# Moving three DMA groups and one cast in a fused attention and feed-forward kernel

## The chip, the cores and the metric

The kernel runs on 1 core of a Trainium2 chip. The metric is the device time of one execution in microseconds (us). A run is described by the median of several executions; one further execution is recorded by the profiler, and its span (first to last instruction) is what the views of the profile divide up.

The core's engines run their own instruction streams in order and wait for each other by semaphores: PE (matrix products; PEld is its weight load), DVE (vector), ACT (activation functions and copies), POOL (casts here) and SP, which in this kernel issues almost all DMA transfers.

## The reference, cut to what matters

```python
# q, k, v: (8, 8, 576, 64) float32; chunks of 64 rows attend to themselves
scores = scale * q_c @ k_c.T ;  attn = softmax(scores) ;  out = attn @ v_c
x = out.transpose(0, 2, 1, 3).reshape(4608, 512)
h = x @ w_in                      # (4608, 2048)
g = 0.5 * h * (1 + erf(h / sqrt(2)))
y = g @ w_out                     # (4608, 512)
```

## The kernel before

**Tiles.** The 4608 rows are cut into nine tiles of 512 rows, `t` = 0 to 8: one per batch entry (its first 512 rows), and a ninth of the 64 rows that are left of each. A tile's path is: load q, k, v; cast to bf16 on POOL; transpose q and k by DMA; scores, exp, product with v and division (attention); transpose x; mm1 (x times `w_in`, then Gelu); mm2 (times `w_out`); store.

**Rounds.** `phase(t, e1, e2)` runs mm1 and then mm2 of tile t. In the dictionaries `e1` and `e2` work on later tiles is hung at named places of it: during round t the attention of tile t + 1 ends (`rows_av`, `rows_x`), the scores of tile t + 2 are made (`quad_S`), and q, k, v of tiles t + 2 and t + 3 are loaded and cast. "Fifth and sixth mm1" are rounds t = 4 and t = 5. All order is written out by hand (`tc.manual_schedule()`): each engine executes in the order in which the program names the instructions.

**Fewer products.** From t = 1 in mm1 and from t = 3 in mm2 the product is done in seven block products instead of eight (a Strassen-Winograd scheme). The sums of blocks that it takes are DVE instructions: `w_in_sums` (L573, L579 to L582) for the weights, `x_sums` (L588, L598) for x, and for h: `h_sums` (L552, L553), `h_third` (L557) and `h_fourth` (L561).

**mm1 from t = 4 to 7** follows the word list `FOUR` (L620) in `mm1_groups`. A digit and a group letter is a block product (four matmuls, L658). `c1`, `c2`, `c3` and `a1`, `a2` are copies of PSUM sums and additions to them (L693, L706, L709) and `g..` the Gelus (L665). The word `c3c` allocates an output-sized tile from `ypool` (L702) for one of these sums, and DVE fills it at L706 (`h_sb<-h_Y`). `ypool` has two buffers under one tag, and mm2 takes two of them per round for its output, `y[0]` and `y[1]`. So the tile of `c3c` in round t + 1 sits in the buffer of `y[0]` of round t, and L706 waits until the stores from `y[0]` have landed.

**mm2 from t = 3** is `mm2_seven` (L742). Its places, in order: `also(0)`; X product; `also(1)`; `h_third`; products into Y; first store (`y[0]`, left half, L773); `h_fourth`; `also(2)`; the product of `s[3]` by `T[3]` into Z (L778) in two halves, with `also((2, 0))` behind the first; second store (`y[1]`, right half, L780); `also(3)`; a product into Y; third store (`y[0]`, right half, L784); `also(4)`; last product; fourth store (`y[1]`, left half, L788). Each store is one DMA issued on SP (L827).

**DMA.** Loads of k are four DMAs of 256 KB (L102), for tile 8 eight DMAs of 128 KB (L106). V is loaded by `load_v_rows` (L115) in two halves by the parity of the head: four DMAs for parity 0 and five for parity 1 (L122); `cast_v_rows` (L200, L206) casts them by one POOL instruction each. `flip` (L189) transposes q or k by DMA, `rows_x` flips x in two parts (L336). SP issues in program order. The program's semaphores for DMA go round eight at a time: each DMA also waits until the eighth DMA before it has landed.

Of the kernel before, what the change touches and what calls it, by code (L numbers as in the profile page):

```python
# [11 lines left out]
def kernel(  # L12
# [15 lines left out]
    B, H, S, D = q.shape  # L28
# [39 lines left out]
    w_t, w_s = {}, {}  # L68
# [46 lines left out]
    def load_v_rows(t, parity=range(2)):  # L115

        if "vf" not in tiles[t]:
            tiles[t]["vf"] = stage_tile()[:].rearrange("p (h n d) -> p h n d", h=H, d=D)
        raw = tiles[t]["vf"]

        def go(to, rows):
            nc.sync.dma_start(to, rows.rearrange("h key d -> key h d"))  # L122
        last = CT // 2 - 1
        if t < B and 0 in parity:
            for n in range(CT // 2):
                go(raw[:, 0::2, n], v[t, 0::2, P * n:P * (n + 1), :])
        if t < B and 1 in parity:
            for n in range(last):
                go(raw[:, 1::2, n], v[t, 1::2, CH + P * n:CH + P * (n + 1), :])
            go(raw[0:CH, 1::2, last], v[t, 1::2, MT - CH:MT, :])  # L130
            go(raw[CH:P, 1::2, last], v[t, 1::2, 0:CH, :])
        if t == B:
            for b in range(B):
                for r in parity:
                    c, n = place(r, b)
                    go(raw[CH * c:CH * (c + 1), r::2, n], v[b, r::2, MT:S, :])
# [60 lines left out]
        DV(st["kt"][:, g * J:(g + 1) * J].rearrange("p n (e j) -> p (n e) j", j=J),  # L197
           raw[:, g * J:(g + 1) * J].rearrange("p j e -> p e j"))

    def cast_v_rows(t, copy):  # L200
        st = tiles[t]
        st["v"] = ld.tile([P, H, CT // 2, D + 1], bf16, tag="v", name="v_nat")
        if t >= FIRSTX:
            nc.gpsimd.memset(st["v"][:, :, :, D:], 1.0)
        for r in range(2):
            copy(st["v"][:, r::2, :, :D], st["vf"][:, r::2])  # L206
# [122 lines left out]
    def rows_x(t):  # L329

        st = tiles[t]
        rows = work.tile([P, G * CT // 2, 2, D], bf16, tag="x_t", name="x_r", bufs=1)
        xT = st["x"][:].rearrange("p g (n e) -> p (g n) e", e=P)

        def flip_rows(b0, b1):
            nc.sync.dma_start_transpose(xT[:, b0:b1], rows[:, b0:b1].rearrange("p b r d -> p (b r d)"))  # L336
        for bank in range(6):
            b0 = NX * (bank // 2)
            ni = min(NX, G * CT // 2 - b0)
            av = st["av"][bank][:, :ni]  # L340
            one = work.tile([P, NX], f32, tag="one", name="one", bufs=2)
            nc.vector.reciprocal(one[:, :ni], av[:, :, D])
            to = rows[:, b0:b0 + ni, bank % 2]
            nc.vector.tensor_tensor(to, av[:, :, :D], one[:, :ni].to_broadcast([P, ni, D]), op=mybir.AluOpType.mult)
            if bank == 1:
                flip_rows(0, NX)
        flip_rows(NX, G * CT // 2)
# [218 lines left out]
    def w_in_sums(kk, groups):  # L566

        w = in_blocks()
        if not w_s:
            own = consts.tile([P, 4, 2, 4, 2, P], bf16, name="w_in_s")  # L570
            w_s["all"] = own
            for n, g in enumerate("abcd"):
                for i in range(4):  # L573
                    w_s[g, i + 1] = own[:, i, :, n]
        TT, add, sub = nc.vector.tensor_tensor, mybir.AluOpType.add, mybir.AluOpType.subtract
        ns, q, e = {"ab": (slice(0, 2), slice(0, 2), 0), "c": (2, 0, 2), "d": (3, 1, 2)}[groups]
        a11, a12, a21, a22 = (w[:, c, kk, r, q, e:e + 2] for r in range(2) for c in range(2))
        s1, s2, s3, s4 = (w_s["all"][:, i, kk, ns] for i in range(4))
        TT(s1, a21, a22, op=add)  # L579
        TT(s2, s1, a11, op=sub)  # L580
        TT(s3, a11, a21, op=sub)
        TT(s4, a12, s2, op=sub)  # L582
# [128 lines left out]
    def w_sums(which):  # L711

        b11, b12 = w_out_sb[:, :FH, :NH], w_out_sb[:, :FH, NH:]
        b21, b22 = w_out_sb[:, FH:, :NH], w_out_sb[:, FH:, NH:]
        for i in (1, 3):
            if i in which:
                pair = wsum.tile([P, 2, FH, NH], bf16, tag="wsum", name="w_t")
                w_t[i], w_t[i + 1] = pair[:, 0], pair[:, 1]
        of = {1: (b12, b11), 3: (b22, b12), 2: (b22, w_t[1]), 4: (b21, w_t.get(2))}
        for i in which:  # L720
            nc.vector.tensor_tensor(w_t[i], *of[i], op=mybir.AluOpType.subtract)
# [172 lines left out]
    def pool_cast_qk(t):  # L894
        pool_cast_q(t)
        pool_cast_k(t)
# [38 lines left out]
    with tc.manual_schedule():  # L935
# [98 lines left out]
        def flips_of(n):  # L1034
            for nm in "qk":
                flip(n, nm)
# [5 lines left out]
        def loads_of_qk(n):  # L1042
            for nm in "qk":
                load_qk(n, nm)
# [14 lines left out]
        for t in range(1, NT):  # L1059
            e1, e2 = {}, {}  # L1060
            n = t + 1
            if n < NT:
                tiles[n]["x"] = xpool.tile([P, G, MT], bf16, tag="x", name="x")
            if t == 1:
                flips_of(2)
                load_v_rows(2, (1,))
                cast_v_rows(2, PO)
                loads_of_qk(3)
                pool_cast_qk(3)
                e1 = {"1a": [lambda: w_in_sums(slice(0, 2), "c")], "p": [lambda: load_v_rows(3)], "end": [lambda: w_sums((1, 3))]}  # L1070
                e2 = one_tile(2, {5: [lambda: act_table(Act.Gelu)],
                                  8: [lambda: flips_of(3), lambda: loads_of_qk(4)]})
            elif t == 2:
                cast_v_rows(3, PO)
                pool_cast_qk(4)
                e1 = {f"i{g}": [lambda g=g: in_order(3, g)] for g in range(G)}
                e1.update({f"w{i}": [lambda i=i: w_sums((i,))] for i in (2, 4)})
                flips_of(4)
                load_v_rows(4)
                load_qk(5, "q")  # L1080
                cast_v_rows(4, PO)
                e2 = one_tile(3, {8: [lambda: load_qk(5, "k")], 14: [lambda: quad_S(4)]})
            elif n < NT:
                def ahead(t=t):
                    if FIRST7 < t < B - 2:
                        load_v_rows(t + 2)
                    if t + 2 < NT:
                        flips_of(t + 2)
                    if t == FIRST7:
                        load_ahead(t, "q")  # L1090
                    if t == B - 1:
                        load_v_rows(B, (1,))
                        cast_v_rows(B, PO)

                def late_v(t=t):
                    load_v_rows(t + 2)
                    cast_v_rows(t + 2, PO)

                def behind(t=t):
                    load_ahead(t, "k")  # L1100
                e1 = {"begin": [ahead]}
                if t + 2 < NT:
                    e1["begin"] = [lambda t=t: pool_cast_k(t + 2), ahead]
                if t + 2 == B:
                    def behind_sums(t=t):
                        nc.gpsimd.tensor_copy(tiles[B]["q"][:, 0, 0, 0, 0:1], tiles[t]["s", 2][:, 0, 0:1])
                        pool_cast_q(B)
                        pool_cast_k(B)
                        ahead()
                    e1 = {"g11b": [behind_sums]}  # L1110
                if t == FIRST7:
                    pool_cast_q(t + 2)
                    e1["tab"] = [lambda: act_table(Act.Gelu)]
                e2 = {1: [lambda: rows_av(n, tiles[n - 1]["Z"]), lambda: rows_x(n)], 2: [], 3: [], 4: [behind, lambda: x_sums(n)]}
                if t == FIRST7:
                    e2[2] += [late_v, lambda: w_in_sums(slice(0, 2), "d")]
                if FIRST7 < t < B - 2:
                    e2[1] += [lambda t=t: cast_v_rows(t + 2, PO)]
                if t == B - 2:
                    e2[1] += [lambda: load_v_rows(B, (0,))]  # L1120
                if t + 3 < NT:
                    if t > FIRST7:
                        e2[1] += [lambda t=t: load_ahead(t, "q")]
                    if t + 3 < B:
                        e2[1] += [lambda t=t: pool_cast_q(t + 3)]
                if n + 1 < NT:
                    e2[1] = [lambda: act_table(Act.Exp)] + e2[1]
                    e2[2 if t == FIRST7 else (2, 0)] = e2[2] + [lambda: quad_S(n + 1), lambda: act_table(Act.Gelu)]
            phase(t, e1, e2, between=last_rows if t == 1 else {})
# [28 lines left out]
```

## Time and profile before

| what | us |
|---|---|
| runs | 272.81, 273.38, 275.05 |
| median of these | 273.38 |
| profiled execution, whole | 275.35 |
| its span | 273.5 |
| PE busy in it | 262.0 |
| DVE busy | 196.5 |
| ACT busy | 185.6 |
| POOL busy | 79.0 |

Matmuls are pipelined, so a matmul's length in the profile is longer than the time it adds; a row of the timeline with four matmuls of 128x256 advances by 0.44 us. The timeline view gives start, length, engine, line, operation, output and inputs, and in brackets how long the engine stood idle before the row and what ended that.

### The profile page before, as it was taken

What the parts mean: (1) busy time and instruction counts of PE and PEld (TensorE: products, weight loads), DVE (VectorE), ACT (ScalarE), POOL (GpSimd) and SP (SyncE); (2) the same over time, 40 slices, a digit from 0 to 9 for tenths busy, and PEclk for the clock granted to TensorE, in tenths of its full rate; (3) what the DMA queues carried; (4) which work ended last, traced back from release to release, by engine and by line L of the source; (5) the groups of instructions that cost most, each with busy time, mean ns of one, the idle gap of its engine ahead of it and who ended that gap; (6) DMA issues with size and microseconds to landing.
All of it is one profiled execution on the core that took longest, in us unless ns stands there. A gap on an engine that the chain in (4) does not pass through costs nothing. (4 is left out here: it accounts for less than half of the span.)

```text
span 273.5 us, 7503 instructions
## 1 busy us (share of the span) xinstructions
PE 262.0 (96%) x3040; PEld 194.6 (71%) x3057; DVE 196.5 (72%) x360; ACT 185.6 (68%) x361; POOL 79.0 (29%) x125
## 2 busy tenths in 40 slices
PE   8799999999999999999999999999999999999993
PEld 2474455467447754678888888888887888888782
DVE  2547574898895999479958965995599559946841
ACT  3438674887967875997679767966895699338600
POOL 2634666450650361430434203510061011000000
PEclk9759999999999999999999999999999999999999
DMA  6999999998969979989999989979977571440005
GB/s 190 267 357 405 395 396 248 244 266 205 319 174 250 263 161 200 281 205 200 239 236 257 217 228 277 210 141 151 238 180 131 115 213 27 76 157 2 1 2 155
DMA packets 128628, 56.60 MB, mean 207 GB/s; under 512 B 104016, under 2 KB 123472, under 8 KB 128592
## 3 DMA queue, kind: packets, MB, share of 16 engines
q1 hardware_dynamic: 128272, 55.59, 80.1%
q8 instruction: 24, 0.39, 0.6%
q10 hardware_dynamic: 320, 0.52, 0.5%
q14 instruction: 12, 0.10, 0.1%
HBM read 36.70 MB, written 9.44 MB: 169 GB/s over the span
## 5 line engine op out<-in xcount | busy, mean ns | idle before, releaser
L658 PEld LDWEIGHTS <-w_in_s 128*128 128x128 bf16 x448 | 43.7, 98 | 7.0 <-issue 0.4
L658 PEld LDWEIGHTS <-w_in_sb 128*128 128x128 bf16 x336 | 32.8, 98 | 6.7 <-issue 0.6
L727 PEld LDWEIGHTS <-h_s 128*128 128x128 bf16 x304 | 29.3, 98 | 4.7 <-DVE h_s L557 1.2
L836 PE MATMUL y_ps<-w_out_sb,h 128*128 128x512 bf16 x137 | 31.4, 379 | 1.0 <-issue 1.0
L156 POOL CAST q_nat<-arrival 128x512 bf16<-128x512 f32 x33 | 20.2, 649 | 39.6 <-DMA arrival<-in_q_dram 38.1
L658 PE MATMUL h_X<-x,w_in_sb 128*128 128x256 bf16 x224 | 31.4, 273 | 0.0
L156 POOL CAST k_nat<-arrival 128x512 bf16<-128x512 f32 x34 | 23.4, 722 | 27.6 <-DMA arrival<-in_k_dram 22.9
L658 PE MATMUL h_Y<-x_t,w_in_s 128*128 128x256 bf16 x224 | 31.1, 272 | 0.2 <-ACT h_a L706 0.2
L727 PEld LDWEIGHTS <-h 128*128 128x128 bf16 x288 | 28.2, 98 | 3.7
L206 POOL CAST v_nat<-arrival 128x1024 bf16<-128x1024 f32 x14 | 15.9, 1136 | 48.1 <-DMA arrival<-in_v_dram 48.1
L727 PE MATMUL y_ps<-w_t,h_s 128*128 128x256 bf16 x208 | 25.1, 273 | 0.7 <-DVE h_s L557 0.7
L836 PEld LDWEIGHTS <-h 128*128 128x128 bf16 x144 | 13.4, 98 | 15.2 <-issue 0.2
L727 PE MATMUL y_ps<-w_out_sb,h 128*128 128x256 bf16 x192 | 22.9, 273 | 0.0
L693 ACT COPY h_Y<-h_X 128x512 f32<-128x512 f32 x28 | 15.8, 581 | 9.8 <-PE h_X L658 9.7
L933 ACT ACT_TABLE_LOAD x16 | 20.5, 1283 | 1.0 <-PEq L1142 0.7
L706 DVE COPY h_a<-h_Y 128x512 f32<-128x512 f32 x8 | 5.5, 690 | 18.1 <-PE h_Y L658 18.1
L665 ACT ACTIVATE h<-h_Y 128x512 bf16<-128x512 f32 x28 | 16.5, 594 | 1.7 <-PE h_Y L658 1.3
L665 ACT ACTIVATE h<-h_X 128x512 bf16<-128x512 f32 x28 | 16.7, 600 | 1.4 <-PE h_X L658 0.8
L235 ACT ACTIVATE pT<-s_ps 128x512 bf16<-128x512 f32 x28 | 14.4, 602 | 4.6 <-PE s_ps L228 4.6
L658 PE MATMUL h_Z<-x_t,w_in_s 128*128 128x256 bf16 x112 | 16.8, 273 | 0.0
L658 PE MATMUL h_Y<-x,w_in_s 128*128 128x256 bf16 x112 | 16.4, 272 | 0.0
L658 PE MATMUL h_Z<-x_t,w_in_sb 128*128 128x256 bf16 x112 | 16.4, 272 | 0.0
(146 smaller groups left out, 495.2 us busy)
## 6 DMA issues: line engine op xcount, KB each, us to landing
out_dram<-y_sb SPq DMA_DIRECT2D x32, 256.0 KB, 3.2
arrival<-in_q_dram SPq DMA_DIRECT2D x7, 1024.0 KB, 6.9
arrival<-in_k_dram SPq DMA_DIRECT2D x24, 256.0 KB, 5.7
arrival<-in_v_dram SPq DMA_DIRECT2D x42, 128.0 KB, 3.0
arrival<-in_moe_w_out_dram SPq DMA_DIRECT2D x4, 1024.0 KB, 12.2
arrival<-in_v_dram SPq DMA_DIRECT2D x8, 256.0 KB, 6.2
arrival<-in_moe_w_in_dram SPq DMA_DIRECT2D x4, 512.0 KB, 6.8
arrival<-in_moe_w_in_dram SPq DMA_DIRECT2D x2, 1024.0 KB, 10.6
```

The lines of the kernel that those rows point to most:

```text
L156: copy(st[nm][:, g].rearrange("p j r d -> p r j d"), st[nm + "f"][:, 2 * g:2 * g + 2])
L206: copy(st["v"][:, r::2, :, :D], st["vf"][:, r::2])
L235: nc.scalar.activation(pT[:].rearrange("p u (c j) -> p u c j", j=J), s_ps[g2][c][:].rearrange("p u (j c) -> p u c j", j=J), Act.Exp, scale ...
L658: nc.tensor.matmul(banks[g + name][:, i], lhs[:, kk, i], rhs[:, kk], start=fresh and i == kk == 0, stop=(kk == 1), skip_group_check=True)
L665: nc.scalar.activation(h[:, j:j + 2, m], src[:], Act.Gelu)
L693: AC(banks[g + "Y"][:], banks[g + "X"][:])
L706: (AC if i == 0 else DV)(sums[g, i][:], banks[g + "Y"][:])
L727: nc.tensor.matmul(out[m], lhs[:, f, m * P:(m + 1) * P], rhs[:, f, :], start=fresh and f == 0 and (m == 0 or len(out) == 3), stop=(f == FH ...
L836: nc.tensor.matmul(y_ps[:], st["h"][:, f, ms * P:(ms + 1) * P], w_out_sb[:, f, :], start=(f == 0), stop=(f == FF - 1))
L933: nc.scalar.activation(act_scratch[:], rest[:, 0:1], func)
```

## The change

Three edits:

1. Round 1: the cast of V of tile 2, the loads of q and k of tile 3 and their casts are named after `w_in_sums(..., "c")` instead of at the head of the round. The cast of V is made to wait for those sums by a copy of one column of `w_in_s` into `v_nat` ahead of it on POOL. By this the loads of q and k also stand behind the store of the last row block of tile 0 on SP.
2. Rounds 4 and 5: only the first half of V of tile t + 2 is loaded ahead of the DMA transposes of q and k; the second half (five DMAs) follows them.
3. Rounds 3, 4 and 5: the loads of k of tile t + 3 (`behind`) are hung at `also(3)` instead of `also(4)`, and so are issued behind the second store of the round and ahead of the third.

```diff
-    def cast_v_rows(t, copy):
+    def cast_v_rows(t, copy, behind=None):
         st = tiles[t]
         st["v"] = ld.tile([P, H, CT // 2, D + 1], bf16, tag="v", name="v_nat")
+        if behind is not None:
+            copy(st["v"][:, 0, 0, 0:1], behind)
...
             if t == 1:
                 flips_of(2)
                 load_v_rows(2, (1,))
-                cast_v_rows(2, PO)
-                loads_of_qk(3)
-                pool_cast_qk(3)
-                e1 = {"1a": [lambda: w_in_sums(slice(0, 2), "c")], "p": [lambda: load_v_rows(3)], "end": [lambda: w_sums((1, 3))]}
+                def behind_sums():
+                    w_in_sums(slice(0, 2), "c")
+                    cast_v_rows(2, PO, w_s["c", 4][:, 0, 0, 0:1])
+                    loads_of_qk(3)
+                    pool_cast_qk(3)
+                e1 = {"1a": [behind_sums], "p": [lambda: load_v_rows(3)], "end": [lambda: w_sums((1, 3))]}
...
                 def ahead(t=t):
                     if FIRST7 < t < B - 2:
-                        load_v_rows(t + 2)
+                        load_v_rows(t + 2, (0,))
                     if t + 2 < NT:
                         flips_of(t + 2)
+                    if FIRST7 < t < B - 2:
+                        load_v_rows(t + 2, (1,))
...
-                e2 = {1: [lambda: rows_av(n, tiles[n - 1]["Z"]), lambda: rows_x(n)], 2: [], 3: [], 4: [behind, lambda: x_sums(n)]}
+                e2 = {1: [lambda: rows_av(n, tiles[n - 1]["Z"]), lambda: rows_x(n)], 2: [], 3: [behind], 4: [lambda: x_sums(n)]}
```

## The prediction, made before the changed kernel ran

> **What bounds the kernel now.** I read the page first (who is busy), then the windows of rounds 4, 5 and 6, then the waits of PE and its weight load, then timelines of DVE, POOL, PE and SP where rounds differ.
>
> ```profile
> PE 262.0 (96%) x3040; PEld 194.6 (71%) x3057; DVE 196.5 (72%) x360; ACT 185.6 (68%) x361; POOL 79.0 (29%) x125
> ```
>
> PE leaves 11.5 us of the span idle, nearly all of it before 45 us, which the change does not touch. Each window below runs from one round's first matmul to the next one's; the first number after the stretch is its length, then PE.
>
> ```profile
> 136.20:162.40 26.20, 26.18 (x354) 23.05 (x352) 19.92 (x40) 19.94 (x38) 6.79 (x10) 1.00 1.01 225
> 162.40:189.20 26.80, 26.44 (x354) 23.00 (x353) 20.39 (x39) 20.68 (x38) 7.36 (x11) 1.00 0.91 211
> 189.20:215.95 26.75, 26.41 (x354) 23.01 (x353) 20.21 (x39) 20.65 (x38) 5.93 (x10) 1.00 0.86 172
> ```
>
> The same 354 matmuls take 26.20, 26.80 and 26.75 us: rounds 5 and 6 lose 0.60 and 0.55 us. The waits view and the timelines say where:
>
> ```profile
> PEld L727 <- DVE h_s L557: 1.2, 2, 0.6
> ...
> 151.62 0.69 DVE L553 TENSOR_TENSOR h_s<-h_s,h 128x1024 bf16<-128x1024 bf16 x1
> ...
> 177.18 0.68 DVE L552 TENSOR_TENSOR h_s<-h 128x1024 bf16<-128x1024 bf16 x1
> 177.90 1.41 DVE L553 TENSOR_TENSOR h_s<-h_s,h 128x1024 bf16<-128x1024 bf16 x1
> ...
> 177.29 1.48 POOL L206 CAST v_nat<-arrival 128x1024 bf16<-128x1024 f32 x1 [1.56 <-DMA arrival<-in_v_dram]
> ...
> 185.18 1.05 PE L727 MATMUL y_ps<-w_t,h_s 128*128 128x256 bf16 x8 [0.34 <-DVE h_s L557]
> ```
>
> In round 5 V's second cast starts at 177.29 inside L552, takes 1.48 us instead of 1.04, and L553 takes 1.41 instead of 0.69 (round 4). DVE is 0.72 late from there, h_third (L557) ends late, and PE waits for it at 185.18. Round 6 has the same with the casts of k: L553 0.98 and L552 0.82 instead of 0.69 and 0.42, and a wait of the same kind. So up to 0.60 + 0.55 = 1.15 us can be won here.
>
> What can be lost stands on SP and DVE at the end of round 5 and in round 6:
>
> ```profile
> 185.36 4.90 SPq L111 DMA_DIRECT2D arrival<-in_q_dram  x8
> 190.68 1.69 SPq L827 DMA_DIRECT2D out_dram<-y_sb  x3
> 192.93 7.18 SPq L106 DMA_DIRECT2D arrival<-in_k_dram  x8
> 200.21 0.57 SPq L827 DMA_DIRECT2D out_dram<-y_sb  x1
> ...
> 199.53 0.68 DVE L706 COPY h_sb<-h_Y 128x512 f32<-128x512 f32 x1
> 200.31 0.69 DVE L709 TENSOR_TENSOR h_sb<-h_Z,h_sb 128x512 f32<-128x512 f32 x1
> 201.15 0.69 DVE L706 COPY h_d<-h_Y 128x512 f32<-128x512 f32 x1
> 201.94 0.69 DVE L709 TENSOR_TENSOR h_d<-h_Z,h_d 128x512 f32<-128x512 f32 x1
> ...
> 202.69 0.60 PE L658 MATMUL h_Z<-x_t,w_in_sb 128*128 128x256 bf16 x4
> ```
>
> L706 at 199.53 (word c3c) refills the buffer of y[0]; in the built programs, before and after, it waits for round 5's first and third stores. Before, the third is issued at 192.00 and lands 5.6 us later, at 197.6: slack 1.9 us. Between L706 and the matmuls at 202.69 DVE has no spare time but 0.15 us ahead of 201.15.
>
> **Part 2, V's second half behind the transposes (rounds 4, 5).** No instruction is added. In round 5 the first half is issued from about 169 to 171.9, the transpose of q follows (1.90 us before) without waiting for five loads, that of k waits for the end of k's cast (174.7 before, about 174 after), then five loads take 2.8 us, to about 179. A V load lands 2.7 to 4.1 us after issue (median 3.0), so the second cast starts at about 181.5 instead of 177.29. There DVE runs rows_x, which reads PSUM; a cast beside it in round 4 (153.42) left both at their usual lengths. The 0.72 us on DVE and PE's wait go: 0.60 less 0.05 that stays (round 5 has a small wait at 175.94 from h1's L553, which meets k's cast), **-0.55 us**. Low end 0 if the cast lands on h_third, high end -0.60. x's flips on SP start when rows_x has made x (181.7 before), behind loads that are out by 179: free. In round 4 the moved loads end at about 154.6, just ahead of x's first flip (154.93 before); landing at 157 or later, the cast meets h_third (156.91 to 158.13) after its start and delays h_fourth, which has 0.6 us spare before its product: 0, at worst +0.7 if it starts just ahead of h_third.
>
> The rows say that one of the two waits: the cast's extra 0.44 us is what L552 had left at 177.29 (to 177.86, less the overlap of one DVE row with the next, about 0.1), and L553 ends 0.7 after the cast. The Trainium skill (SBUF — State Buffer, Who interferes with whom) has it as an exclusive lock: a DVE instruction with two SBUF inputs and a GpSimd one that reads SBUF block each other for a whole instruction. The trace agrees with its 1.48 and 1.41; by that rule, too, the one-PSUM-input rows_x is free, and a cast just ahead of h_third would cost a whole 1.04 us there, less 0.35 us of slack.
>
> **Part 3, k one store sooner (rounds 3, 4, 5).** k lands sooner by what one store takes of the queue, about 0.7 us; POOL's casts of k start that much sooner, PE needs them a round later: 0. But the third store now stands behind the k loads. Round by round, on the clock of before:
>
> - Round 3 into 4: SP is issue-bound there; four k loads take 3.45 us (row at 140.03), so the third store goes from 139.56 to 142.95 and lands just ahead of where the fourth landed (147.6): about 146.7. c3c of round 4 is due at 146.49: 0.2 late, less 0.15: **+0.1**, bounds 0 and +0.9 (at 147.6).
> - Round 4 into 5: from 163.93 to 166 or 167, landing at 171.5 (it must land before the fourth, 172.7), due at 173.02: 0.
> - Round 5 into 6: the tile-8 loads wait for q, eight DMAs back. The third store and first three k loads started at 192.00, 192.93, 193.92, 194.97, each as a q load landed. After, k loads 1 to 4 take these four starts; the last one is 0.87 long, and loads 5 to 8 at the median of 0.63 end at 198.4 (at their own former lengths 199.4). The third store follows: 198.4 to 199.4. Since rows_x, the flips and q move 0.7 sooner, 197.7 to 198.7. Landing 2.9 us later, as the fourth did behind the k loads at 200.21: 200.6 to 201.6. c3c is due at 199.53 - 0.55 = 199.0. Late by 1.6 to 2.6; I take 2.1, less 0.15, **+1.95**. Bounds: landing after 2.3 us (shortest store of the trace) and starting at 197: 0.3 late; at the former landing of the fourth store, 203.1, which stood behind the same transfers: 4.1 late on paper, 3.6 if that moves with the rest.
>
> A transfer issued later moving later is also what the Trainium skill says (DMA: Bandwidth & Descriptors, Queues, rings and completion order): on each DMA engine descriptors are consumed in ring order. The rows agree: the four stores of round 5 landed in the order of issue, behind q.
>
> With DVE 2 us late in round 6, its h sums meet no k casts, which the gate on h1 (L1106, 199.74) starts ahead of the wait: **-0.45** of the 0.55.
>
> **Part 1, round 1.** The copy costs POOL 0.19 us (row L1106). V's first cast moves from 57.98 to about 60.5; before, it stretched the fourth x sum to 1.14 from 0.41 us. PE's small waits there (0.14 us at 59.57, 0.08 at 60.09) end with copies on ACT, not DVE, so I take 0; bounds -0.3 and +0.2. Behind the cast on POOL are q and k of tile 3, which wait for loads until 70.7. The store goes 2.5 us sooner, the 1 MB loads of q and k 0.7 later; their transposes are issued at 80.98, 4 us after k's cast: 0.
>
> **Sum.** -0.55 + 0.1 + 0 + 1.95 - 0.45 + 0 = +1.05, and 0.1 for k's casts meeting h1 in round 5: +1.15. The profiled execution took 275.35 (273.5 and 1.85 around it), 1.97 over the median of 273.38; it would become 276.5, the median **274.5**.
>
> **The rivals.**
>
> - *Faster: the third store of round 5 still lands in time.* One point decides: its landing against 199.0. It needs an issue by 196.1 at 2.9 us. For: eight loads of bare 0.6 us from 191.3 end at 196.1. Against: four of them wait for q. Then -0.55 - 0.5 and the rest 0: 272.4.
> - *Several stores late and a cast on h_third:* 3.4 in round 6, 0.7 in round 4 and no gain in round 5: about +3.3, 276.7. For: 5.6 us is how long the store took before; against: that was with q's megabyte ahead of it.
> - *Nothing to see:* the wait in round 6 is 0.8 and pays off the two gains: 273.4. For: the low end 0.3; against: it needs the shortest landing and earliest issue together.
>
> **How the numbers follow.** Forecast (late by 1.3 to 3) 0.62; faster rival 0.16; nothing 0.12; worse rival 0.10. The forecast's own range is 273.9 to 275.6; to leave out 2 in 10 the range reaches from 272.5 to 276.0. A measurement of this kernel can tell about 1% (2.7 us) from no change: faster by that needs more than the 1.15 us that can be won, 0.03; slower is the worse rival and a little of the forecast, 0.12; within 1% 0.85.
>
> **What would show it.** Right: in round 5 L553 at 0.69 and no PE wait for L557; in round 6 an idle stretch of about 2 us on DVE ahead of L706 h_sb put down to a store, and a PE wait of that size in the same words; L552 and L553 of round 6 at 0.42 to 0.69. Wrong: no DVE idle at c3c (the faster rival), or V's second cast beside L557.

## The result, and the profile after

The changed kernel takes 276.36 us, the median of ten runs (273.82 to 277.77); the kernel before, run beside it on the same chip, 273.11 us (median of ten, 272.07 to 275.05). The ratio of the runs is 1.0106, with a 95% interval from 1.0069 to 1.0143: the change costs 1.9 to 3.9 us, about 2.9. The forecast was 274.5 and its range ended at 276.0.

The profiled execution of the changed kernel took 276.03 us (span 274.2). It is only 0.7 us longer than the profiled execution of the kernel before, because that one had spent 2.0 us more ahead of round 4 (which began at 136.20 us there, and at 134.20 us here). So the rounds are compared one by one. The windows of rounds 4, 5 and 6, as in the prediction: stretch, length, then PE, PEld, DVE, ACT and POOL.

```profile
134.20:161.28 27.08, 26.50 (x355) 23.04 (x353) 20.80 (x40) 20.07 (x37) 7.29 (x10) 1.00 1.03 217
161.28:187.87 26.59, 26.31 (x355) 23.07 (x353) 20.33 (x39) 20.75 (x38) 7.57 (x11) 1.00 0.95 216
187.87:216.87 29.00, 26.63 (x355) 23.06 (x352) 19.47 (x39) 20.72 (x38) 4.90 (x10) 1.00 0.75 158
```

Against 26.20, 26.80 and 26.75 before this is +0.88, -0.21 and +2.25: 2.92 us together, as much as the runs differ. That they agree so closely is chance: second profiles of both kernels (e11 and e12 below) differ by 1.63 us in these rounds. Round 7 takes 25.46 us in both. (A window's edge is the first recorded product of a round; one record more or less moves it by 0.04 us.)

The waits view of the changed kernel has two rows that were not there before, and the row of the weight load waiting for `h_third` is gone. The columns are total us, times, longest:

```profile
DVE h_sb L708 <- DMA out_dram<-y_sb: 3.4, 2, 2.9
...
PE h_Y L660 <- DVE h_sb L708: 1.8, 1, 1.8
```

The lines of the program have moved by two: L708 is the old L706, L711 the old L709, L554 and L555 the old L552 and L553, L559 the old L557 (`h_third`). The timeline view of the changed kernel, first SP at the end of round 5, then DVE and PE in round 6:

```profile
188.80 1.24 SPq L829 DMA_DIRECT2D out_dram<-y_sb  x2
190.47 7.40 SPq L106 DMA_DIRECT2D arrival<-in_k_dram  x8
197.97 1.09 SPq L829 DMA_DIRECT2D out_dram<-y_sb  x2
...
197.81 0.42 DVE L555 TENSOR_TENSOR h_s<-h_s,h 128x512 bf16<-128x512 bf16 x1
201.16 0.69 DVE L708 COPY h_sb<-h_Y 128x512 f32<-128x512 f32 x1 [2.92 <-DMA out_dram<-y_sb]
201.96 0.69 DVE L711 TENSOR_TENSOR h_sb<-h_Z,h_sb 128x512 f32<-128x512 f32 x1
...
201.91 0.60 PE L660 MATMUL h_Y<-x,w_in_s 128*128 128x256 bf16 x4 [1.79 <-DVE h_sb L708]
202.70 0.60 PE L660 MATMUL h_Z<-x_t,w_in_sb 128*128 128x256 bf16 x4 [0.20 <-DVE h_sb L711]
...
204.09 0.60 PE L660 MATMUL h_Z<-x_t,w_in_sb 128*128 128x256 bf16 x4 [0.36 <-DVE h_d L711]
```

The third store of round 5 is issued at 197.97, behind eight loads of k, and lands at 200.97, 3.0 us later. `c3c` (L708) follows 0.2 us behind the landing; DVE had been idle for 2.92 us, and PE stops three times. (The bracket gives PE's idle time; what a stop costs is read from the starts: four products advance by 0.44 us, and from 199.51 to 201.91 it is 2.40, so 1.96 lost, then 0.36 and 0.52. That is 2.84; 0.06 of it stands in undisturbed rounds too, which leaves 2.78.) In round 5 the same row shows a wait of 0.51 us, and the h sums have their undisturbed length again (L555 0.69 us, against 1.41 before):

```profile
172.16 0.69 DVE L708 COPY h_sb<-h_Y 128x512 f32<-128x512 f32 x1 [0.51 <-DMA out_dram<-y_sb]
...
176.33 0.68 DVE L554 TENSOR_TENSOR h_s<-h 128x1024 bf16<-128x1024 bf16 x1
177.04 0.69 DVE L555 TENSOR_TENSOR h_s<-h_s,h 128x1024 bf16<-128x1024 bf16 x1
```

In round 4 `c3c` is late too, though its row names PE:

```profile
145.56 0.69 DVE L708 COPY h_sb<-h_Y 128x512 f32<-128x512 f32 x1 [1.00 <-PE h_X L660]
```

The third store of round 3 was issued at 141.49 and landed 3.9 us later, at 145.37; `c3c` starts 0.2 us behind that, as it does behind the landings in rounds 5 and 6. So this wait is read as one for the store as well.

V's second cast of round 5 did not land beside `rows_x`, where it was forecast, but 0.46 us after `h_third` had begun. The timeline view of the changed kernel, POOL and DVE:

```profile
182.80 1.66 POOL L208 CAST v_nat<-arrival 128x1024 bf16<-128x1024 f32 x1 [7.22 <-DMA arrival<-in_v_dram]
...
182.34 1.21 DVE L559 TENSOR_TENSOR h_s<-h 128x2048 bf16<-128x2048 bf16 x1
```

Here `h_third` keeps its length and PE does not wait for it. In other executions the order is the other way round (e12 below).

### The profile page after: what moved, and what is told of

It is laid out like the page before. It is cut to its first block, busy times and chain, and to the rows that moved or that the text cites. A ratio compares the mean times of both kernels' runs of the same rounds, so it can differ in the third digit from the quotient of the medians.

```text
span 274.2 us, 7502 instructions
## 1 busy us (share of the span) xinstructions
PE 258.5 (94%) x3040; PEld 192.3 (70%) x3057; DVE 197.3 (72%) x360; ACT 185.8 (68%) x361; POOL 79.7 (29%) x126
## 4 chain that ended last, share of the span: by engine, by line
PE 82%; SPq 5%; DMA 5%; DVE 2%; issue 2%; ACT 1%; POOL 1%; DVEq 0%; ACTq 0%; POOLq 0%
PE y_ps L729 24%; PE h_Y L660 12%; PE y_ps L838 11%; PE h_Z L660 9%; PE h_X L660 8%; DMA arrival<-in_moe_w_in_dram 4%; PE y_ps L863 4%; PE y_ps L738 3%; PE h_ps L682 3%; PE h_ps L521 2%; SPq L141 2%; SPq L908 2%; PE s_ps L230 2%; SPq L108 1%; PE av_ps L326 1%
## 5 line engine op out<-in xcount | busy, mean ns | idle before, releaser
L156 POOL CAST q_nat<-arrival 128x512 bf16<-128x512 f32 x33 | 22.5, 720 | 38.7 <-DMA arrival<-in_q_dram 37.2
L156 POOL CAST k_nat<-arrival 128x512 bf16<-128x512 f32 x34 | 20.7, 647 | 21.9 <-DMA arrival<-in_k_dram 17.8
L708 DVE COPY h_a<-h_Y 128x512 f32<-128x512 f32 x8 | 5.5, 691 | 17.6 <-PE h_Y L660 17.6
## 6 DMA issues: line engine op xcount, KB each, us to landing
arrival<-in_moe_w_in_dram SPq DMA_DIRECT2D x2, 1024.0 KB, 10.6
```

Source lines behind the costliest of these rows:

```text
L156: copy(st[nm][:, g].rearrange("p j r d -> p r j d"), st[nm + "f"][:, 2 * g:2 * g + 2])
```

## The experiments

The theory: part 3 alone makes the loss, because the third store is issued late behind the loads of k and `c3c` of the next round waits for it. The rival: the moved loads of V, the moved cast, or the traffic itself costs. "r4, r5, r6" are the lengths of rounds 4 to 6 in the one profiled execution of each kernel; ratios are to the kernel before, run in the same group on the same chip. `h1`, `h2` and `h3` are the words of the list `FOUR` at which `h_sums` runs (L552, L553): `h1` just ahead of `c3c`, `h2` and `h3` at the end of mm1.

| kernel | r4 | r5 | r6 | sum | ratio (95%) |
|---|---|---|---|---|---|
| before | 26.20 | 26.80 | 26.75 | 79.75 | 1 |
| before, again (e11) | 26.66 | 26.95 | 26.68 | 80.29 | |
| changed | 27.08 | 26.59 | 29.00 | 82.67 | 1.0106 (1.0069 to 1.0143) |
| changed, again (e12) | 26.51 | 26.89 | 28.52 | 81.92 | |
| e1 parts 1 and 2 | 26.70 | 26.67 | 26.75 | 80.12 | 0.9973 (0.9943 to 1.0002) |
| e2 part 3 | 27.02 | 27.18 | 29.70 | 83.90 | 1.0114 (1.0074 to 1.0154) |
| e3 part 2 | 26.76 | 26.44 | 26.60 | 79.80 | 1.0036 (1.0003 to 1.0070) |
| e4 part 1 | 26.88 | 26.67 | 26.35 | 79.90 | 0.9978 (0.9948 to 1.0009) |
| e5 own buffer | 26.82 | 26.92 | 26.87 | 80.61 | 1.0023 (0.9989 to 1.0057) |
| e6 store on ACT | 26.23 | 26.28 | 26.23 | 78.74 | 0.9994 (0.9958 to 1.0029) |
| e6 again (e10) | 28.40 | 26.68 | 26.24 | 81.32 | |
| e7 k of tile 8 behind | 28.69 | 26.89 | 26.35 | 81.93 | 1.0060 (1.0025 to 1.0095) |
| e8 half of k ahead | - | - | - | - | 1.0036 (0.9998 to 1.0074) |
| e9 before, gated | 26.23 | 26.23 | 26.50 | 78.96 | 0.9950 (0.9918 to 0.9983) |
| e13 own buffer, gated | 26.24 | 26.76 | 26.33 | 79.33 | 0.9984 (0.9957 to 1.0012) |
| e14 before, gated in 4, 5 | 26.23 | 26.24 | 26.33 | 78.80 | 0.9966 (0.9939 to 0.9993) |

26.23 us is what a round takes when PE waits for nothing but what it waits for in every round.

**e1, parts 1 and 2 alone.**

```diff
-2: [], 3: [behind], 4: [lambda: x_sums(n)]}
+2: [], 3: [], 4: [behind, lambda: x_sums(n)]}
```

> The changed kernel with the loads of k back behind the third store (parts 1 and 2 alone). Theory (the loss is the late third store alone): the word c3c waits for no store, rounds 4, 5 and 6 last about 26.2, 26.3 and 26.3 to 26.8 us, no wait for h_third in round 5; the median is 0.3 to 1.0 us below the kernel before, some 272.5. Rival (V's five moved loads or the moved cast cost time, by themselves or on the DMA queue): slower than before by 1 us or more, with a wait for V, for a transpose or for x somewhere in rounds 4 to 6.

No wait of `c3c` for a store, and by the ratio the kernel is 0.7 us below the kernel before, just within what could be chance. So the loss is not in these parts. But rounds 4 and 5 took 0.4 to 0.5 us more than expected: casts of k met the h sums of `h1`, and PE waited 0.5 us in each round.

**e2, part 3 alone** (the same line, on the kernel before).

> The kernel before with only the loads of k moved ahead of the third store (part 3 alone). Theory: the third stores of rounds 3, 4 and 5 land late, c3c waits, and rounds 4, 5 and 6 lose about 0.8, 0.4 and 2.3 us more than before; median about 3 to 3.5 us above the kernel before (276.1 to 276.6), since part 2's gain of 0.5 is missing. Rival (the store is late only together with V's moved loads): c3c on time in round 6, the median within 0.7 us of before.

The theory holds for the whole and for round 6: the ratio is that of the whole change, without any of V's moves. The timeline view of e2 in round 6:

```profile
189.38 7.91 SPq L106 DMA_DIRECT2D arrival<-in_k_dram  x8
197.38 1.08 SPq L827 DMA_DIRECT2D out_dram<-y_sb  x2
...
200.46 0.69 DVE L706 COPY h_sb<-h_Y 128x512 f32<-128x512 f32 x1 [3.61 <-DMA out_dram<-y_sb]
```

The eight loads hold SP for 7.91 us here, and the wait is 3.61 us. Round 4 took 0.82 us more than before, as expected, but for another reason: `c3c` waits for no store there (it starts as soon as `h1`'s sums end), and PE's waits come from `h1`'s sums and from `h_third`, which casts had stretched.

**e3, part 2 alone.**

```diff
-                        load_v_rows(t + 2)
+                        load_v_rows(t + 2, (0,))
                     if t + 2 < NT:
                         flips_of(t + 2)
+                    if FIRST7 < t < B - 2:
+                        load_v_rows(t + 2, (1,))
```

> The kernel before with only V's second half behind the transposes (part 2 alone). Theory: the first h sum of DVE (its second instruction) takes 0.69 instead of 1.41 us in round 5 and PE's wait for h_third there goes; 0.5 us shorter round 5, the others unchanged, median 0.3 to 0.7 us below before. Rival (the cast finds another DVE instruction to meet): round 5 at 26.8 as before, median equal.

Between the two: PE's wait in round 5 is gone, as forecast, but one of the same size stands in round 4, and the median is above the kernel before. The timeline view of e3 in round 4 shows V's first cast, which the change does not move, beside an h sum:

```profile
148.46 1.41 DVE L553 TENSOR_TENSOR h_s<-h_s,h 128x1024 bf16<-128x1024 bf16 x1
...
147.90 1.43 POOL L206 CAST v_nat<-arrival 128x1024 bf16<-128x1024 f32 x1 [0.80 <-DMA arrival<-in_v_dram]
```

**e4, part 1 alone** (round 1 of the changed kernel, the rest as before).

> The kernel before with only round 1 changed (part 1 alone). Theory: nothing, within 0.3 us of before; rounds 4 to 6 as before. Rival (the loads of q and k of tile 3, asked for later, or the cast of V, waiting for the sums, hold up round 1 or 2): 1 us or more slower, with the time lost between 55 and 110 us.

By the ratio it is 0.6 us below, within chance. Nothing is lost in round 1; the small waits stand in other rounds once more (26.88 in round 4).

**e5, a buffer of its own for `c3c`** (in the changed kernel, rounds 4 to 7).

```diff
-                    pair = ypool.tile([P, 4, TH], f32, tag="y", name="h_sb")
+                    if four:
+                        sums[g, 1] = work.tile([P, 2, TH], f32, tag="y_2", name="h_sb", bufs=1)
+                    else:
+                        pair = ypool.tile([P, 4, TH], f32, tag="y", name="h_sb")
```

> The changed kernel with the tile of c3c in rounds 4 to 7 taken from the work pool (a 2 KB buffer that mm2's sum y_2 leaves idle then) instead of from ypool. The third store is as late as in the changed kernel, but no instruction of DVE waits for it. Theory (the loss is the wait of c3c for the buffer): rounds 4, 5 and 6 together take 79.7 to 80.2 us as in the runs without the wait, not 82.7, and the median is 2.5 to 3.3 us below the changed kernel, about level with the kernel before or up to 0.8 below. Rival (the late stores or k's early loads also cost through DMA traffic, casts or the transposes): it stays 1 us or more above the kernel before.

The stores are as late as in the changed kernel (the third is issued at 197.02, behind 7.11 us of k loads), and nothing waits for them: 80.61 us instead of 82.67, and 1.0023 instead of 1.0106. With the stores as late and only the buffer changed, the loss is gone: it goes through the buffer. The sum is 0.4 us above the upper end of what was expected. The timeline view of e5 has `c3c` of round 6 (L710 there) without a wait, and in round 5 an h sum that stood behind V's first cast:

```profile
197.75 0.68 DVE L710 COPY h_sb<-h_Y 128x512 f32<-128x512 f32 x1
...
174.99 1.56 DVE L554 TENSOR_TENSOR h_s<-h 128x1024 bf16<-128x1024 bf16 x1
...
174.97 1.04 POOL L208 CAST v_nat<-arrival 128x1024 bf16<-128x1024 f32 x1 [1.50 <-DMA arrival<-in_v_dram]
```

**e6, the third store issued on ACT** (rounds 3 to 5), and **e10**, the same kernel once more.

```diff
-        nc.sync.dma_start(out[m0:m0 + TH, cols]...
+        (nc.scalar if (th, nh) == (0, 1) and t < 6 else nc.sync).dma_start(out[m0:m0 + TH, cols]...
```

> The changed kernel with the third store of rounds 3 to 5 issued on ACT, whose instruction fills its source, instead of on SP behind the k loads. Theory (the store is late because it is issued late, behind loads that each wait for an older transfer): it is issued as soon as ACT has copied, some 5 us earlier in round 5, and lands about 3 us later; c3c is on time, rounds 4 to 6 together 79.7 to 80.5 us (an issue on ACT may cost some tenths), median within 1 us of the kernel before. Rival (the store is late because the rings of the DMA engines are filled with the data of q and k): it still lands after 199 in round 5's terms, c3c waits 1.5 us or more, and the median stays 2 us above the kernel before.

> The changed kernel with the third store on ACT a second time, one look. Theory: no wait of c3c for a store again; rounds 4 to 6 take 78.7 to 79.8 us, according to which sums the ungated casts meet in this execution. Rival (it was luck that the store landed in time): c3c waits for a store by 0.5 us or more in one of the rounds.

In e6 `c3c` waits in no round, and the three rounds are nearly as short as they can be. The timeline view of e6, SP and ACT at the end of round 5 (it began its round 6 at 185.87):

```profile
187.36 0.38 ACTq L829 DMA_DIRECT2D out_dram<-y_sb  x1
...
186.85 1.94 SPq L829 DMA_DIRECT2D out_dram<-y_sb  x2
193.11 6.75 SPq L106 DMA_DIRECT2D arrival<-in_k_dram  x8
```

The store leaves 8.6 us sooner than in the changed kernel (1.5 us into round 6 instead of 10.1). It is not the whole story, though. In the built program the first of the k loads uses the semaphore that this store used last, and waits for its landing. By that the store took some 5.7 us, not the 3 that were expected (the profile shows no landing for it), and k starts 7.2 us into round 6, against 2.6 in the changed kernel and 3.7 before: k is later, not sooner, and its casts fall behind the h sums. Round 7 takes 25.78 us instead of 25.46, and the ratio is no better than before. e10 shows what can happen instead: the timeline view, ACT and then PE at the start of round 4.

```profile
132.60 0.58 ACT L785 COPY y_sb<-y_ps 128x512 f32<-128x512 f32 x1 [0.20 <-PE y_ps L729]
136.06 0.46 ACTq L829 DMA_DIRECT2D out_dram<-y_sb  x1
136.57 1.06 ACT L695 COPY h_Y<-h_X 128x512 f32<-128x512 f32 x2 [3.38 <-DMA arrival<-in_v_dram]
...
137.19 0.60 PE L660 MATMUL h_Y<-x_t,w_in_s 128*128 128x256 bf16 x4 [1.56 <-ACT h_Y L695]
```

Now ACT is the engine that waits for an older transfer, a load of V, before it may issue the store. The copy behind it comes late and PE loses 1.7 us: 28.40 us in round 4. Neither the theory nor the rival of e10 had this.

**e7, only the loads of k of tile 8 behind the third store again**, and **e8, four of the eight**.

```diff
-3: [behind], 4: [lambda: x_sums(n)]}
+3: [behind] if t < 5 else [], 4: [lambda: x_sums(n)] if t < 5 else [behind, lambda: x_sums(n)]}
```

> The changed kernel with only round 5's loads of k (tile 8, eight loads) back behind the third store; rounds 3 and 4 (four loads each) keep them ahead of it. Theory (the size of the loss goes with the loads issued ahead of the store): the wait of c3c in round 6 goes and takes 2.3 to 2.9 us with it; rounds 4 and 5 keep their waits of 0.4 to 0.8 us; median 0.3 to 1.0 us above the kernel before. Rival (a single store late by its place in the ring of eight DMA semaphores costs as much in every round): rounds 4 and 5 lose 1.5 us or more each.

> The changed kernel with only the first four of round 5's eight loads of k ahead of the third store, the other four behind it. Theory (each load ahead delays the issue by what it takes itself, 0.6 to 1 us): the third store is issued about 3 us sooner than in the changed kernel and lands at or just ahead of what c3c needs; the wait in round 6 is 0 to 0.5 us and the median 0.3 to 1.2 us above the kernel before. Rival (one wait for an old transfer among the first loads makes the delay, whatever their number): the wait in round 6 stays at 2 us or more.

In e7 round 6 is at 26.35: with the loads gone from ahead of it, the loss of round 6 goes. Round 4, however, lost 2.46 us against the 26.23, three times what it had in the changed kernel, though the program up to there is the same, and the ratio stands at +1.6 us instead of the 0.3 to 1.0 expected. The timeline view of e7, round 3 into 4 (which began at 133.35):

```profile
128.00 3.06 SPq L338 DMA_TRANSPOSE x<-x_r  x1
...
131.74 5.97 SPq L122 DMA_DIRECT2D arrival<-in_v_dram  x9
...
138.41 3.69 SPq L102 DMA_DIRECT2D arrival<-in_k_dram  x4
142.20 1.28 SPq L829 DMA_DIRECT2D out_dram<-y_sb  x2
...
146.33 0.69 DVE L708 COPY h_sb<-h_Y 128x512 f32<-128x512 f32 x1 [2.61 <-DMA out_dram<-y_sb]
```

The third store is issued 8.85 us into round 4, against 7.29 in the changed kernel, 6.21 in e2 and 6.14 in e12. Of the 1.56 us between e7 and the changed kernel, the flip of x takes 0.95 (3.06 us against 2.11), the four loads of k 0.38 (3.69 against 3.31), and the flip started 0.25 later in its round; V's nine loads take the same. `c3c` is due 10.3 us into the round, and the store lands 3.6 to 3.9 us behind its issue there. So in e2 and e12 it lands in time, and the 0.3 us that round 4 still loses in e12 is `h1`'s sums beside casts of k (0.64 and 0.71 us instead of 0.42); in the changed kernel `c3c` starts 1.1 us late and in e7 2.7. The loss through the store in round 4 is 0 to 2.4 us by what SP meets in that execution. e7's rival, 1.5 us or more in rounds 4 and 5, holds for round 4 of this execution and not for round 5, which lost 0.66.

e8's profiled execution is one of its longest (277.92 us against a median of 275.49), so its round lengths are left out of the table, and it is read for what happens around the third store. The timeline view, SP at the end of round 5 (round 6 began at 190.73):

```profile
193.38 3.69 SPq L106 DMA_DIRECT2D arrival<-in_k_dram  x4
197.17 0.83 SPq L829 DMA_DIRECT2D out_dram<-y_sb  x1
198.04 3.83 SPq L106 DMA_DIRECT2D arrival<-in_k_dram  x4
```

Four loads ahead hold the store for 3.7 us instead of 7.4; it goes 6.4 us into the round instead of 10.1, and lands 4.5 us later, at about 201.6. `c3c` starts at 201.72, 0.7 us late, and PE loses 0.5 us. So with none of the eight loads ahead (e7) `c3c` of round 6 is on time, with four it is 0.7 us late, with eight 2.5 to 3.7 (e12, the changed kernel, e2): the size of the wait goes with the number of loads, as far as one execution with four can show it.

**e11 and e12, both kernels once more.**

> The kernel before a second time, one look. If the small waits of PE behind h sums depend on where loads happen to land, they stand in other rounds than in the first profile, and rounds 4, 5 and 6 differ from 26.20, 26.80 and 26.75 by up to 0.6 us each, their sum by less than 0.8 us. If they are set by the program, the three lengths repeat within 0.1 us.

> The changed kernel a second time, one look. Theory: c3c waits for the third store in round 6 again, 2.5 to 3.5 us, round 6 takes 28.5 to 29.7 us; the wait in round 4 is anywhere from 0 to 2.6 us, as in the runs that share its rounds 3 and 4. Rival (the wait of round 6 is an accident of one execution): under 1 us.

Round 4, free of waits for h sums in the first profile of before, loses 0.4 us in e11. The small waits depend on when a load happens to land; over the three rounds they come to 1.1 and 1.6 us in the two profiles. In e12 `c3c` of round 6 waits again, 2.4 us, just under what was expected, and in round 4 it waits for no store. In round 5 V's second cast begins 0.28 us ahead of `h_third`, and PE loses 0.4 us (POOL, DVE, PE):

```profile
201.63 0.69 DVE L708 COPY h_sb<-h_Y 128x512 f32<-128x512 f32 x1 [2.43 <-DMA out_dram<-y_sb]
...
182.59 1.04 POOL L208 CAST v_nat<-arrival 128x1024 bf16<-128x1024 f32 x1 [6.39 <-DVE x_r L346]
...
182.87 1.84 DVE L559 TENSOR_TENSOR h_s<-h 128x2048 bf16<-128x2048 bf16 x1
...
184.77 1.05 PE L729 MATMUL y_ps<-w_t,h_s 128*128 128x256 bf16 x8 [0.25 <-DVE h_s L559]
```

e7 has the same order in round 5 (the cast at 182.70, `h_third` at 183.01 for 1.80 us).

**e9 and e14, the kernel before with its casts gated**: one-column copies on POOL hold the casts of k behind `h1` and those of V behind `h3` in rounds 4 and 5; e9 also holds k of tile 8 in round 6, and its transpose, behind `h3`. The lines of e14:

```diff
+                if FIRST7 < t < B - 2:
+                    def behind_h1(t=t, ahead=ahead):
+                        nc.gpsimd.tensor_copy(tiles[t + 2]["k"][:, 0, 0, 0, 0:1], tiles[t]["s", 2][:, 0, 0:1])
+                        pool_cast_k(t + 2)
+                        ahead()
+                    e1 = {"g11b": [behind_h1]}
...
-                    e2[1] += [lambda t=t: cast_v_rows(t + 2, PO)]
+                    e2[1] += [lambda t=t: cast_v_rows(t + 2, PO, tiles[t]["s", 2][:, 6, 0:1])]
```

> The kernel before, none of the three parts; instead POOL's casts in rounds 4 to 6 are held by one-column copies until the h sums are done: k behind h1, V of rounds 4 and 5 and k of tile 8 behind h3. Theory (PE's waits of 0.4 to 0.6 us in these rounds come from casts that run beside DVE sums with both inputs in SBUF): the h sums run at 0.41 to 0.69 us in all three rounds, rounds 4 to 6 take 78.7 to 79.1 us together as in the run with the store on ACT, against 79.8 in the profile before; median 0.5 to 1.2 us below the kernel before. Rival (a cast held back makes a transpose late, k of tile 8 above all): PE waits for k_t at the scores of round 6, 0.5 us or more, and the median is not below the kernel before.

> The kernel before with the same gating of rounds 4 and 5 alone, round 6 untouched. Theory: rounds 4 and 5 at 26.2, round 6 at 26.3 to 26.8 by where the casts of k of tile 8 land, round 7 at 25.5 (not 26.1 as with round 6 gated); median 0.5 to 1.3 us below the kernel before. Rival (the gain of e9 came from round 6's gate, or from chance): not below before.

In both, rounds 4 and 5 take the 26.23 us that the casts theory says, and both are below the kernel before, by 0.5% (0.2 to 0.8) and 0.3% (0.1 to 0.6, so just clear of zero). e9's rival is there too, in small: its held k makes PE wait 0.3 us for `k_t` in round 6, and its round 7 takes 26.06 instead of 25.46 us; e14, without that gate, has 25.47. So rounds 4 to 7 explain 0.2 to 0.7 us of e9's 1.4 (against the two profiles of before), and 0.9 to 1.5 us in e14, whose ratio says 0.9.

**e13, `c3c` in its own buffer and the gates of e14, on the changed kernel.**

> The changed kernel with c3c's tile in its own buffer (as in e5) and, in rounds 4 and 5, the casts of k held behind h1 and those of V behind h3. Theory (what e5 still lost against the shortest rounds is casts beside h sums): rounds 4 and 5 take 26.2 to 26.3 us each, round 6, where k is not held, 26.2 to 26.9; median 0 to 1.2 us below the kernel before. Rival (late stores or V's second half behind the transposes cost by themselves): rounds 4 or 5 stay at 26.6 or more though the h sums have their usual lengths.

Round 4 is free and round 5 is not, though its h sums have their usual lengths: here the rival has a point. The timeline view of e13 in round 5:

```profile
178.61 1.93 DVE L559 TENSOR_TENSOR h_s<-h 128x2048 bf16<-128x2048 bf16 x1
...
178.42 1.04 POOL L208 CAST v_nat<-arrival 128x1024 bf16<-128x1024 f32 x1 [2.19 <-DMA arrival<-in_v_dram]
```

V's second cast, late because its loads stand behind the transposes, starts just ahead of `h_third` (L559), which ends 0.71 us late; PE waits 0.51 us. That is a price of part 2, the one seen in e12 and e7.

## Why the prediction was wrong

The place, the mechanism and the sign were right: the third store behind the loads of k, `c3c` waiting for its buffer, PE waiting for `c3c` with no more than about 0.15 us of slack. Its sum for rounds 4 to 6 was +1.15; the profile has +2.92. Of the 1.8 us between them 0.8 lie in round 6, 0.7 in round 4 and 0.3 in round 5. By its steps, as the first profile of the changed kernel has them:

- **Part 3, round 5 into 6: the term that was mis-sized most.** Forecast: late by 2.1, +1.95. Measured: `c3c` 13.29 us into the round instead of 10.33, 2.96 late, and PE's three stops cost 2.78 (3.5 in e2, 2.3 in e12). The landing time (3.0 us, taken as 2.9) was right. The first k load started 7.7 us ahead of when `c3c` was due, exactly as forecast. The size that failed is SP's time from there to the store: "loads 5 to 8 at the median of 0.63" made 6.4 us, "at their own former lengths" 7.4, and the middle, 6.9, was taken. It is 7.5 in the changed kernel (190.47 to 197.97), 8.0 in e2 and 7.9 in e12, at or beyond the far end. The waits for q were not it: they come to 1.3 us in the changed kernel as before (SP's waits view). It is the issues themselves: loads 5 to 8 took 0.89, 0.63, 1.34 and 0.64 us, much as before (0.92, 0.63, 1.27, 0.64), and e2 and e12 have one of 1.5 us among them too. A median for four loads left the long ones out. Of the rest, 0.2 us lie between the landing and the start of `c3c`, and 0.1 in the landing.
- **Round 3 into 4.** Forecast +0.1, bounds 0 and 0.9. Measured 0.8, and through the store 0 (e2, e12) to 2.4 (e7) in other executions with the same moves there. The issue time was worked out from one execution as if SP repeated it; ahead of that store SP has two flips, nine loads of V, two stores and four loads of k, some of which wait for an older landing, and e7 lies far beyond the bound.
- **Round 4 into 5.** Forecast 0; `c3c` waited 0.51 us and PE's small stop in that round grew from 0.11 to 0.42 us: +0.3. The store landed 171.98 - 161.28 = 10.7 us into the round, where 10.3 was needed. Its issue, 4.6 us into the round, was as forecast; the landing took 6.1 us, where 171.5 had left 4.5 to 5.5. In e2, e12 and e7 it landed at 10.6 to 10.7 too.
- **Part 2.** Forecast -0.55: the cast lands at about 181.5, beside `rows_x`. In this profile PE's wait for `h_third` in round 5 did go (0.51 us), as did L553's 1.41, but by luck. The cast came 21.5 us into the round instead of 19.1, beside `h_third`, which the prediction names as a sign of being wrong; it fell behind the start of `h_third` by 0.46 us. The five loads behind the transposes began 1.5 us later in the round than forecast: the first four loads of V were through 0.7 later, and q's transpose took 2.72 us, not 1.90. In e12 and e7 the cast comes first and the gain is lost: the forecast's low end, 0. Besides, the step took one execution's collision for the program's: e11 shows the kernel before with the waits elsewhere, e3 shows part 2 with a new one in round 4. What part 2 costs alone stays open: 0 to 1.9 us by e3, while e1, which contains it, has -1.6 to +0.1 us.
- **Part 3 in round 6, the h sums.** Forecast -0.45; the second wait for `h_third` (0.49 us) went, in the changed kernel, e12 and e2. The reason given fits: DVE is late, and its sums have their usual lengths.
- **Part 1.** Forecast 0; e4 cannot tell it from 0. The +0.1 for k's casts beside `h1` in round 5 did not come in this profile: both sums took their 0.42 us.

Of the rivals, "several stores late" was the nearest: it gave 276.7 us, with 3.4 in round 6, and the stores did come late in three rounds. (Its listed terms make +4.1, or +3.65 with the 0.45 of round 6, and not the +3.3 it names.) Its other half, 0.7 us for a cast on `h_third` in round 4, did not happen in this profile: that cast started at 156.33, after `h_third` had (155.75). For round 5 it did in e12, e7 and e13.

Open: what makes the flip of x and the loads on SP in round 3 longer or shorter from one execution to the next was not tried; nor was a version that leaves round 3 as it was. The lengths of rounds are one or two executions of each kernel: in e12 the loss of round 6 is 2.3 us, not far from the +1.95.

## What to carry to other kernels

A DMA that frees a buffer is on the path of whoever refills that buffer; before loads are issued ahead of it, add up what those loads hold the issuing engine for, the long ones at their own lengths and each with its wait for older transfers, and compare with when the refill is due. A wait seen once in one profile may be an accident of landing times: look whether its cause is fixed by the program before its removal is counted as a gain; here holding the casts in order (e9, e14) won 0.3 to 0.5%, which moving their loads did not. Moving the store to another engine moves the wait along with it, and an engine that also computes (ACT in e10) pays for it at once.

## What the runs showed of the hardware

- A DVE sum with both inputs in SBUF that starts beside a cast on POOL runs when the cast has ended: in e5 the cast ends at 176.01 (174.97 and 1.04) and L554, which needs 0.68, ends at 176.55; in e13 the cast ends at 179.46 and `h_third`, which needs 1.22, at 180.54. The Trainium skill (SBUF — State Buffer, Who interferes with whom) calls this an exclusive lock, with the one who comes first keeping it for the whole instruction; these rows agree, to the 0.1 us or so by which DVE rows overlap.
- The same in the other order: in the changed kernel `h_third` starts first (182.34) and keeps its 1.21 us, and the cast that starts at 182.80 takes 1.66 us instead of 1.04.
- Issuing eight loads of 128 KB held SP for 7.2 us before, 7.4 in the changed kernel and 7.8 and 7.9 in e12 and e2; waits for older transfers were 1.0 to 1.3 us of that, and in each of the four one load alone took 1.3 to 1.5 us to issue, against a median of 0.63 in the kernel before and the changed one.
- What a store of 256 KB takes to land is not fixed by what stands just ahead of it. Behind loads of k it took 3.0 us in round 5 of the changed kernel, 3.9 in round 3 and 6.1 in round 4; before, behind q's megabyte, 5.6. On ACT's queue it seems no quicker: in e6 it was issued at 187.36, and the first k load, which waits for it, started at 193.11.
